# A convolution and two dense layers on one core: five blocks of the first layer ahead of the second, sums kept in DRAM, some additions by DMA

## The chip, the cores and the metric

The kernel runs on 1 core of a Trainium2 chip. The metric is device time in microseconds (us) of one execution; lower is better. The profiled execution has a trace with every instruction of the engines (TensorE or PE, VectorE or DVE, ScalarE or ACT, GpSimd or POOL) and every DMA; SP issues most DMAs. "Granted clock" is the share of TensorE's full clock (2.4 GHz) that it was granted; the lower level is 1.2 GHz.

## The reference

```python
# x: (2, 4096, 192), weight_gen: (2, 4096, 8, 7); w_in: (192, 2048), w_out: (2048, 192), two of each; weights as 64-bit numbers
w = softmax(weight_gen, axis=-1)                       # 7 taps for each of 8 heads of 24 channels
out = einsum('bshk,bskhg->bshg', w, last_7_rows_of_x)  # a causal local sum
x1 = out.reshape(8192, 192)
h = x1 @ w_in1;  x2 = maximum(0.01 * h, h) @ w_out1    # first layer
h = x2 @ w_in2;  r = maximum(h, 0);  return (r * r) @ w_out2   # second layer
```

The x and the weight_gen are float32, the weights come as 64-bit numbers, which the kernel converts itself.

## The kernel before

The 8192 tokens are cut into 16 blocks (`tb`) of 512. Each block goes through a local sum (softmax of the taps, seven products with shifted rows of x, six additions), then the first layer, then the second. A layer is 8 steps (`j`), each for two chunks of 128 hidden units: `mm1` makes the hidden sums of both chunks (18 products, L491), `activate` applies the nonlinearity on ACT and splits the result into a rounded part `gh` and a rest `gl` (DVE, L516), and `mm2` multiplies both with `w_out` (20 products, L533), two steps later (`LAG`). Every operand is such a pair of rounded part and rest, so each product is taken three times. The contraction over 192 channels is done by two halves of the array with 64 rows each; so a block's input is kept as `a` (channels 0 to 127), `b` (channels 128 to 191, twice) and `s` (`a` with its halves swapped), each with its rest: six tiles, `XS`, and three sets of them.

Layers alternate: `phases` is (layer 0, block 0), then (0, 1), (1, 0), (0, 2), (1, 1) and so on. At the end of a first-layer block, `end1` adds the two halves' sums (`total`, ACT copy L554, DVE addition L557), exchanges halves by DMA and makes the six tiles of the second layer at once. At the end of a second-layer block, `end2` adds, transposes and stores the output.

The weights are converted in `piece`: a DMA load of the 64-bit words (`raw`), an ACT scaling (L261), five DVE instructions (L265 to L287) that put the high and the low word together, the last of them the addition of L287, an ACT copy for the rounded part (L299) and a DVE subtraction for the rest (L304). Each matrix is converted in pieces of one or two steps' worth (384 or 768 columns of 128 partitions): five pieces for each first-layer matrix, four for each second-layer one.

`local_sum` for blocks 0 and 1 (`EARLY`) ends in transposes on TensorE into PSUM, three groups (`a`, `b`, `s`); for later blocks it ends in a DVE transpose, a round trip through DRAM (`sc`) and a `swap` by DMA for `s`. Its buffers `xc`, `wg` and `att` exist once.

What sets the order: every operation is entered in a `Plan` with an engine, an estimated cost, a priority (counted in steps), and what it reads and writes. `issue` is a list scheduler that runs once while the program is built: for each engine it takes, among the next 60 by priority, the one that can start first by the estimates (TensorE strictly by priority), and writes the instructions in that order. Each engine then runs its instructions in this fixed order, so one that waits on the chip holds up those behind it. `late` is the estimate for a DMA. Rings (`buf`) are buffers that a plan entry takes when it is issued; `raw` has 2, the wide scratch tiles `w` 4, the tiles `c` 3.

Of the kernel before, what the change touches and what calls it, by code (L numbers as in the profile page):

```python
# [37 lines left out]
class Plan:  # L38
# [10 lines left out]
    def op(self, eng, cost, prio, reads, writes, fn, after=(), late=0.0):  # L49
        deps = set(after)  # L50
        for b in reads:
            deps.update(b.writers)
        for b in writes:
            deps.update(b.readers or b.writers)
        o = Op(eng, cost, fn, prio, deps, [], late)
        for b in dict.fromkeys([*reads, *writes]):
            o.bufs.append(b)
            b.left += 1
        for b in reads:
            b.readers.append(o)  # L60
        for b in writes:
            if b.readers:
                b.writers, b.readers = [], []
            b.writers.append(o)
        self.ops.append(o)
        return o

    def issue(self, gap=0.07):
# [28 lines left out]
        while left:  # L97
# [31 lines left out]
            if o.late:  # L129
                wire = max(wire, s + o.cost) + o.late  # L130
                o.end = wire + 2.0
# [10 lines left out]
def kernel(  # L142
# [17 lines left out]
    nc = tc.nc  # L160
# [20 lines left out]
    LAG = 2  # L181
    EARLY = 2
# [22 lines left out]
    ident_b = Buf()  # L205

# [16 lines left out]
    def piece(kind, l, j, nj, pr):  # L223
        n = nj * 3 * P
        raw = pl.buf(sb, [P, SW, 2], I32, "raw", "raw", 2)
        wu = pl.buf(sb, [P, SW], F32, "wu", "w", 4)
        wa = pl.buf(sb, [P, SW], F32, "wa", "w", 4)
# [5 lines left out]
        if kind == "i":  # L233
            src = (w_in1, w_in2)[l].rearrange("(s p) (n e m) w -> p s n e (m w)", p=Q, e=2, m=P)
            for d in range(2):
# [6 lines left out]
                pl.op("SP", 0.5 * nj, pr - 6, [], [raw], load, late=nj * 0.7)  # L242
        else:
# [7 lines left out]
            pl.op("SP", 0.5, pr - 6, [], [raw], load, late=nj * 1.4)  # L251
# [4 lines left out]
        def I(b):  # L256
# [4 lines left out]
            lambda: nc.scalar.activation(V(wu), raw.t[:, :n, 1].bitcast(F32), AF.Copy, scale=2.0**-112),  # L261
        )
# [34 lines left out]

        hb = Buf()
        pl.op("ACT", act(n), pr - 1, [wa], [hb], lambda: nc.scalar.copy(hi, val()))  # L299
        parts = [(lo, slice(None))] if kind == "i" else [(lo[:, :, Q:], slice(0, P)), (lo[:, :, :Q], slice(P, D))]  # L300
        for to, cs in parts:
            pl.op(
                "DVE", dve(n // len(parts)), pr - 1, [wa, hb], [done],
                lambda to=to, cs=cs: nc.vector.tensor_tensor(  # L304
                    to, val()[:, :, cs], hi[:, :, cs].bitcast(F32), op=ALU.subtract
                ),
            )

# [20 lines left out]
    x1 = []  # L329
    taken = []  # L330

    def swap(xs, pr):
        for k in "hl":
# [6 lines left out]
            pl.op("SP", 1.0, pr, [xs["a" + k]], [xs["s" + k]], go, late=1.0)  # L340

    AW = 5 * Q

    def local_sum(tb, pr, gate=()):
# [5 lines left out]
        xs = x_set()  # L350
        x1.append(xs)
# [3 lines left out]
        def load_w():  # L355
            for i in range(BI):
                nc.sync.dma_start(
# [3 lines left out]
        def load():  # L361
            q = nc.sync if tb else nc.scalar
# [11 lines left out]
        pl.op("SP", 2.0, pr - 10, [], [wg], load_w, after=gate, late=0.4)  # L374
        pl.op(*(("SP", 2.0) if tb else ("ACT", 4.0)), pr - 10, [], [xc], load, after=gate, late=3.6)
# [23 lines left out]
        c0 = Q if tb < EARLY else 0  # L399

        def acc():
            return att.t[:, :, c0 : c0 + D].rearrange("p t (h g) -> p t h g", g=G)
# [6 lines left out]
        for k in range(1, K):  # L409
            tmp = pl.buf(sb, [P, TB, H, G], F32, "tmp", "c", 3)  # L410
            pl.op("DVE", dve(TB * D), pr - 2, [xc, wg], [tmp], lambda k=k, tmp=tmp: prod(k, tmp.t))
            pl.op(
                "DVE", dve(TB * D), pr - 2, [att, tmp], [att],
                lambda tmp=tmp: nc.vector.tensor_tensor(acc(), acc(), tmp.t, op=ALU.add),  # L414
            )

        def halves(k, v, bufs, dep, pr):
            h, lo = xs[k + "h"], xs[k + "l"]
            pl.op("ACT", act(N), pr, [dep], [h], lambda: nc.scalar.copy(h.t, v()))
            pl.op(  # L420
                "DVE", dve(N), pr, [dep, h], [lo],
                lambda: nc.vector.tensor_tensor(lo.t, v(), h.t.bitcast(F32), op=ALU.subtract),
            )

        if tb < EARLY:

            def copies():
                nc.scalar.copy(
                    att.t.rearrange("p t (c e) -> p t c e", e=Q)[:, :, 0:5:4],
                    att.t.rearrange("p t (c e) -> p t c e", e=Q)[:, :, 2:4],  # L430
                )

            pl.op("ACT", act(N), pr - 1, [att], [att], copies)
            for k, o in (("a", Q), ("b", 3 * Q), ("s", 0)):
# [8 lines left out]
                halves(k, lambda pt=pt: pt.t[:, 0, :], None, pt, pr - 1)  # L443
        else:
            J = D // 32
            xb = pl.buf(sb, [P, J, TB, 32], F32, "xb", "c", 3)
# [9 lines left out]
                lambda: nc.sync.dma_start(out=sc.t, in_=xb.t.rearrange("p j t a -> p (j t a)")), late=1.5,  # L456
            )
            for k, js in (("a", (0, 1, 2, 3)), ("b", (4, 5, 4, 5))):
# [9 lines left out]
                pl.op("SP", 2.0, pr - 2, [sc], [v, *xs.values()], back, after=taken[max(tb - 2, 0) : max(tb - 1, 0)], late=1.2)  # L468
                halves(k, lambda v=v: v.t, None, v, pr - 1)
# [3 lines left out]
    x2 = []  # L473
# [4 lines left out]
    def mm1(l, tb, j, pr):  # L478
        xs = (x1, x2)[l][tb]
        ph = h_t[l, tb, j] = pl.buf(ps, [P, 2, N], F32, "ph", "ph", 2)  # L480

        def go():
            wh, wl = wi[l]["h"], wi[l]["l"]
            slots = ("asb", "sab")
            terms = [(wh, "h", s) for s in (0, 1, 2)] + [(wl, "h", s) for s in (0, 1, 2)]
            terms += [(wh, "l", s) for s in (0, 1, 2)]
            for i, (w, hl, s) in enumerate(terms):

                for d in range(2):
                    c = s if d == 0 else (1, 0, 2)[s]  # L490
# [3 lines left out]
                        rhs=xs["asb"[s] + hl].t[HALVES[d]],  # L494
# [66 lines left out]
    def wide(name):  # L561
        return pl.buf(sb, [P, N], F32, name, "w", 4)

    def end1(tb, acc, pr):
        xs = x_set()
        x2.append(xs)
        sa, bs, bw = wide("sa"), wide("bs"), wide("bw")
        taken.append(total(acc, 0, sa, [*xs.values()], pr))
        total(acc, 1, bs, [bw], pr)

        def other():
            nc.sync.dma_start(out=bw.t[0:Q], in_=bs.t[Q:P])
            nc.sync.dma_start(out=bw.t[Q:P], in_=bs.t[0:Q])

        pl.op("SP", 1.0, pr, [bs], [bw], other, late=1.0)
        ah, al, bh, bl = (xs[k] for k in ("ah", "al", "bh", "bl"))
        pl.op("ACT", act(N), pr + 1, [sa], [ah], lambda: nc.scalar.copy(ah.t, sa.t))
        pl.op(
            "DVE", dve(N), pr + 1, [sa, ah], [al],
            lambda: nc.vector.tensor_tensor(al.t, sa.t, ah.t.bitcast(F32), op=ALU.subtract),  # L580
        )
        swap(xs, pr + 1)
        pl.op(
            "DVE", dve(N), pr + 2, [bs, bw], [bs], lambda: nc.vector.tensor_tensor(bs.t, bs.t, bw.t, op=ALU.add)
        )
        pl.op("ACT", act(N), pr + 2, [bs], [bh], lambda: nc.scalar.copy(bh.t, bs.t))
        pl.op(
# [97 lines left out]
```

## Time and profile before

| | us |
|---|---|
| median of 2 runs (1237.59 to 1239.06) | 1238.32 |
| profiled execution, its own time | 1238.8 |
| its span, first to last instruction | 1236.8 |
| TensorE busy | 1163.9 |
| VectorE busy | 741.5 |
| ScalarE busy | 746.6 |
| GpSimd busy | 1.7 |

The span is what the trace covers; the time of the execution is 2.0 us longer. Busy time is an average over stages with different limits: the page's row of 40 slices (30.9 us each) and the windows show each stretch by itself. A wait is listed with who ended it.

### The profile page before, as it was taken

To read this page: it belongs to the slowest core of one execution; us is meant where nothing else is said; L and a number is where in the kernel's file an instruction comes from. 1 tells how busy PE (TensorE), PEld (TensorE's weight loads), DVE (VectorE), ACT (ScalarE), POOL (GpSimd) and SP (SyncE) were. 2 spreads that over 40 slices of the span, in tenths; PEclk is the share of its full clock that TensorE was granted. 3 is DMA by queue.
4 is the path that set the end of the run, shared out by engine and by line. 5 is a ranking of instruction groups with operands and counts; after the bars stand their busy time and mean duration, and the time that the engine had idled before them with its cause. 6 is when DMAs were issued, how large, how long until landed. Compare 5 with 4: busy or idle time off the path is not lost.

```text
span 1236.8 us, 22770 instructions
## 1 busy us (share of the span) xinstructions
PE 1163.9 (94%) x9752; PEld 932.6 (75%) x9752; DVE 741.5 (60%) x886; ACT 746.6 (60%) x826; POOL 1.7 (0%) x7
## 2 busy tenths in 40 slices
PE   1569889999999999999999999999999999999997
PEld 0457668888888787878878787887878788787885
DVE  6899988747383754738374573738456473433333
ACT  1446665765647566564757566475756657475674
POOL 0000000000000000000000000000000000000000
PEclk9879979999999999999999999999999999999999
DMA  4454253321213131122313112131312211111111
GB/s 91 120 127 122 73 119 69 99 51 35 67 35 92 35 92 36 42 51 49 79 35 92 35 48 51 42 79 35 92 35 64 45 32 43 35 27 18 27 18 18
DMA packets 99532, 72.77 MB, mean 59 GB/s; under 512 B 58156, under 2 KB 84810, under 8 KB 99432
## 3 DMA queue, kind: packets, MB, share of 16 engines
q1 hardware_dynamic: 99120, 70.36, 24.6%
q8 instruction: 76, 1.25, 0.4%
q10 hardware_dynamic: 312, 0.97, 0.3%
q14 instruction: 24, 0.20, 0.1%
HBM read 37.47 MB, written 11.80 MB: 40 GB/s over the span
## 4 chain that ended last, share of the span: by engine, by line
PE 91%; DVE 6%; DMA 1%; ACT 1%; issue 0%; SPq 0%; DVEq 0%; ACTq 0%
PE ph L491 43%; PE pa L533 29%; PE pb L533 19%; DVE att L414 1%; DVE tmp L406 1%; DVE gl L516 1%; DMA raw<-in_moe_w_in_dram 1%; DVE wu L281 0%; DVE wa L271 0%; DVE wa L287 0%; DMA xa<-sc 0%; DVE wu L277 0%; DVE wa L265 0%; DMA xc<-in_x_dram 0%; DVE wo L304 0%
## 5 line engine op out<-in xcount | busy, mean ns | idle before, releaser
L516 DVE TENSOR_TENSOR gl<-g,gh 128x1024 fp32r<-128x1024 f32 x256 | 313.3, 1224 | 412.2 <-ACT g L513 273.8
L533 PE MATMUL pa<-gh,wo 64*128 64x512 f32 x2048 | 285.1, 397 | 7.7 <-DVE sa L557 7.7
L508 ACT ACTIVATE gh<-ph 128x1024 fp32r<-128x1024 f32 x128 | 131.6, 1028 | 258.6 <-PE ph L491 258.5
L533 PEld LDWEIGHTS pa<-gh,wo 64*128 64x128 f32 x2048 | 194.1, 186 | 58.0 <-DVE sa L557 8.5
L511 ACT ACTIVATE g<-ph 128x1024 f32<-128x1024 f32 x128 | 131.6, 1028 | 152.3 <-PE ph L491 151.7
L533 PE MATMUL pa<-gl,wo 64*128 64x512 f32 x1024 | 162.8, 395 | 4.1 <-DVE gl L516 4.1
L533 PE MATMUL pb<-gh,wo 64*128 64x512 f32 x1024 | 162.3, 394 | 3.8 <-DVE bs L557 3.8
L533 PE MATMUL pb<-gl,wo 64*128 64x512 f32 x1024 | 162.6, 395 | 0.0
L513 ACT ACTIVATE g<-g 128x1024 f32<-128x1024 f32 x128 | 135.9, 1062 | 3.6
L512 ACT ACTIVATE gh<-g 128x1024 fp32r<-128x1024 f32 x128 | 135.8, 1061 | 3.6
L509 ACT ACTIVATE g<-ph 128x1024 f32<-128x1024 f32 x128 | 130.5, 1020 | 0.5 <-DVE gl L516 0.5
L533 PEld LDWEIGHTS pa<-gl,wo 64*128 64x128 f32 x1024 | 97.3, 186 | 27.6 <-DVE gl L516 4.6
L533 PEld LDWEIGHTS pb<-gh,wo 64*128 64x128 f32 x1024 | 97.2, 186 | 27.4 <-DVE bs L557 4.5
L533 PEld LDWEIGHTS pb<-gl,wo 64*128 64x128 f32 x1024 | 97.5, 186 | 23.3
L414 DVE TENSOR_TENSOR att<-att,tmp 128x768 f32<-128x768 f32 x96 | 91.7, 955 | 2.0
L406 DVE TENSOR_TENSOR tmp<-xc,wg 128x768 f32<-128x768 f32 x96 | 91.3, 951 | 0.0
L491 PE MATMUL ph<-xah,wi0h 64*128 64x512 f32 x256 | 52.8, 408 | 14.5 <-ACT wi0h L299 14.5
L491 PE MATMUL ph<-xah,wi0l 64*128 64x512 f32 x256 | 52.8, 408 | 4.6 <-DVE wi0l L304 4.6
L491 PE MATMUL ph<-xsh,wi0l 64*128 64x512 f32 x256 | 52.3, 404 | 0.0
L491 PE MATMUL ph<-xbh,wi0l 64*128 64x512 f32 x256 | 52.3, 404 | 0.0
L491 PE MATMUL ph<-xsh,wi0h 64*128 64x512 f32 x256 | 52.2, 403 | 0.0
L491 PE MATMUL ph<-xal,wi0h 64*128 64x512 f32 x256 | 52.0, 402 | 0.0
(90 smaller groups left out, 1461.0 us busy)
## 6 DMA issues: line engine op xcount, KB each, us to landing
xc<-in_x_dram SPq DMA_DIRECT2D x60, 240.0 KB, 4.3
xsh<-xah SPq DMA_DIRECT2D x60, 128.0 KB, 2.4
xsl<-xal SPq DMA_DIRECT2D x60, 128.0 KB, 2.4
raw<-in_moe_w_in_dram SPq DMA_DIRECT2D x32, 192.0 KB, 4.0
raw<-in_moe_w_out_dram SPq DMA_DIRECT2D x7, 768.0 KB, 4.5
sc<-xb SPq DMA_DIRECT2D x14, 384.0 KB, 2.4
bw<-bs SPq DMA_DIRECT2D x32, 128.0 KB, 2.3
out_dram<-ta SPq DMA_DIRECT2D x64, 64.0 KB, 2.1
```

The lines of the kernel that those rows point to most:

```text
L406: nc.vector.tensor_tensor(dst, xk, wg.t[:, :, :, k : k + 1].to_broadcast([P, TB, H, G]), op=ALU.mult)
L414: lambda tmp=tmp: nc.vector.tensor_tensor(acc(), acc(), tmp.t, op=ALU.add),
L491: nc.tensor.matmul(ph.t[:, d, :], lhsT=w[HALVES[d], c, j, :], rhs=xs["asb"[s] + hl].t[HALVES[d]], start=(i == 0), stop=(i == len(terms) - 1),)
L508: pl.op("ACT", W, pr, [ph], [gh], lambda: nc.scalar.activation(gh.t, ph.t, AF.Prelu, alpha=0.01))
L509: pl.op("ACT", W, pr, [ph], [g], lambda: nc.scalar.activation(g.t, ph.t, AF.Prelu, alpha=0.01))
L511: pl.op("ACT", W, pr, [ph], [g], lambda: nc.scalar.activation(g.t, ph.t, AF.Relu))
L512: pl.op("ACT", W, pr, [g], [gh], lambda: nc.scalar.activation(gh.t, g.t, AF.Square))
L513: pl.op("ACT", W, pr, [g], [g], lambda: nc.scalar.activation(g.t, g.t, AF.Square))
L516: lambda: nc.vector.tensor_tensor(gl.t, g.t, gh.t.bitcast(F32), op=ALU.subtract),
L533: nc.tensor.matmul(acc[d][w == "b"].t, lhsT=wt[:, {"ah": slice(0, P), "b": slice(P, 2 * P), "al": slice(2 * P, 3 * P)}[w]], rhs=g.t[HALVES ...
```

## The change

1. Order of the layers: `LEAD = 5`. The first five phases are layer 0 of blocks 0 to 4, then (1, 0), (0, 5), (1, 1), (0, 6) and so on; the last five phases are all of layer 1.
2. `end1` only adds and stores the sums to DRAM (`ka`, `kb`). A new `again` reads them back one phase ahead of the second layer (`b` twice by four DMAs in place of the exchange) and makes the six tiles.
3. Second-layer weight tiles are allocated where the first layer's staging buffers (`raw0` with 4, `w0` with 8) were, in a pool that is closed first; so the first write of second-layer weights waits for all of the first layer's conversion (`borrowed`). Second-layer pieces have priorities 16 steps early, and each loads after the piece two before it and starts after the one before it (`gate=one[-2:]`).
4. For all pieces of the first layer but the first of each matrix, the addition of L287 becomes a DMA with `accum_op=ALU.add`, issued by POOL (`plus`); in block 1's local sum so do five of the six additions of L414.
5. Blocks 0 and 1 make `s` by two products with a permutation matrix and two ACT copies (`turn`), in place of the third group of transposes, ACT copy and DVE subtraction.
6. First block: x is loaded by SP and weight_gen by ACT, where it was the other way round. Block 1's local sum has its priority 6 steps ahead of its phase, it was 1.
7. `mm1` takes the terms of `a` and `b` first and those of `s` last. Scratch tiles `c` 2 for 3, the output sums have a ring `e` of their own. The estimates `late` become pairs (time on the wire, further delay) with other values.

The diff, cut to its core:

```diff
+    LEAD = 5
-    wi = [{k: const.tile([P, 3, NPR, P], F32R, name=f"wi{l}{k}") for k in "hl"} for l in range(2)]
-    wo = [const.tile([P, NFC, 2 * D], F32R, name=f"wo{l}") for l in range(2)]
+    weight_tiles(const, 0)
+    stage = ExitStack()
+    sg = stage.enter_context(tc.tile_pool(name="sg", bufs=1))
+    borrowed = []
+    def second():
+        if len(wi) == 1:
+            stage.close()
+            weight_tiles(ctx.enter_context(tc.tile_pool(name="const2", bufs=1)), 1)
+    def plus(to, tv, of, ov, pr, late):
+        pl.op(
+            "POOL", 1.0, pr, [of, to], [to],
+            lambda: nc.gpsimd.dma_start(out=tv(), in_=ov(), accum_op=ALU.add), late=late,
+        )
-    def piece(kind, l, j, nj, pr):
+    def piece(kind, l, j, nj, pr, dma=False, gate=()):
+        pool, rings = (sb, (("raw", 2), ("w", 4))) if l else (sg, (("raw0", 4), ("w0", 8)))
...
-        pl.op(
-            "DVE", dve(n), pr - 2, [wu, wa], [wa],
-            lambda: nc.vector.tensor_tensor(V(wa), V(wa), V(wu), op=ALU.add),
-        )
+        if dma:
+            plus(wa, lambda: V(wa), wu, lambda: V(wu), pr - 2, (nj * 0.8, 4.5))
+        else:
+            pl.op(
+                "DVE", dve(n), pr - 2, [wu, wa], [wa],
+                lambda: nc.vector.tensor_tensor(V(wa), V(wa), V(wu), op=ALU.add),
+            )
+        pl.op("ACT", act(n), pr - 1, [wa], [hb], high, after=tuple(borrowed) if l else ())
...
+    def turn(xs, pe, pr):
+        pt = pl.buf(ps, [P, 2, N], F32, "pt", "ph", 2)
+        for i, k in enumerate("hl"):
+            pl.op(
+                "PE", MM, pe + 0.1 * i, [xs["a" + k], perm_b], [pt],
+                lambda i=i, k=k: nc.tensor.matmul(pt.t[:, i, :], lhsT=perm, rhs=xs["a" + k].t, start=True, stop=True),
+            )
+        for i, k in enumerate("hl"):
+            pl.op("ACT", act(N), pr, [pt], [xs["s" + k]], lambda i=i, k=k: nc.scalar.copy(xs["s" + k].t, pt.t[:, i, :]))
...
-                nc.sync.dma_start(
+                (nc.sync if tb else nc.scalar).dma_start(
                     out=wg.t[i * A : (i + 1) * A].rearrange("p t h k -> p (t h k)"), in_=wg_flat[i, :, tb]
-            q = nc.sync if tb else nc.scalar
+            q = nc.sync
...
+            if tb == 1 and k < K - 1:
+                plus(att, flat, tmp, lambda tmp=tmp: tmp.t.rearrange("p t h g -> p t (h g)"), pr - 2, (1.6, 4.5))
+            else:
+                pl.op(
+                    "DVE", dve(TB * D), pr - 2, [att, tmp], [att],
+                    lambda tmp=tmp: nc.vector.tensor_tensor(acc(), acc(), tmp.t, op=ALU.add),
+                )
...
+            terms = [(w, hl, s) for ss in ("ab", "s") for w, hl in ((wh, "h"), (wl, "h"), (wh, "l")) for s in ss]
...
     def end1(tb, acc, pr):
+        kept[tb] = [pl.buf(dram, [P, N], F32, n, n, LEAD + 2) for n in ("ka", "kb")]
+        for i in range(2):
+            v, to = wide("s", ("e", 2)), kept[tb][i]
+            total(acc, i, v, [], pr)
+            pl.op("SP", 0.5, pr, [v], [to], lambda v=v, to=to: nc.sync.dma_start(out=to.t, in_=v.t), late=(0.8, 2.0))
+    def again(tb, pr, gate):
+        o = pl.op(
+            "SP", 0.5, pr - 2, [ka], [sa, *xs.values()], lambda: nc.sync.dma_start(out=sa.t, in_=ka.t),
+            after=(taken[-1], *gate), late=(0.8, 2.0),
+        )
+        def twice():
+            for v, rows in ((bu, slice(0, Q)), (bl_, slice(Q, P))):
+                for d in range(2):
+                    nc.sync.dma_start(out=v.t[HALVES[d]], in_=kb.t[rows])
+        halves(xs, "a", lambda: sa.t, sa, pr - 1)
+        swap(xs, pr - 1)
+        pl.op(
+            "DVE", dve(N), pr - 1, [bu, bl_], [bu],
+            lambda: nc.vector.tensor_tensor(bu.t, bu.t, bl_.t, op=ALU.add),
+        )
+        halves(xs, "b", lambda: bu.t, bu, pr - 1)
...
-    phases = [(0, 0)]
-    for tb in range(1, NTB):
-        phases += [(0, tb), (1, tb - 1)]
-    phases.append((1, NTB - 1))
+    phases = [(0, tb) for tb in range(LEAD)]
+    for tb in range(NTB):
+        phases.append((1, tb))
+        if tb + LEAD < NTB:
+            phases.append((0, tb + LEAD))
...
-            piece(kind, l, j, n, at[l, 0] + j + (LAG if kind == "o" else 0))
+            o = piece(
+                kind, l, j, n, at[l, 0] + j + (LAG if kind == "o" else 0) - 16 * l, dma=l == 0 and j > 0, gate=one[-2:] if l else ()
+            )
+            if l:
+                one.append(o)
...
-                    local_sum(tb + 1, at[0, tb + 1] - (4 if tb else 1), gate=() if tb == 0 else (starts[0, tb - 1],))
+                    if lq:
+                        again(tq, at[lq, tq] - 3, gate)
+                    else:
+                        local_sum(tq, at[lq, tq] - (4 if tq >= EARLY else 6), gate)
```

## Rows read from the trace of the kernel before

**Rows 1.** The page, parts 1 and 2: busy times, and DVE's forty slices.
```profile
PE 1163.9 (94%) x9752; PEld 932.6 (75%) x9752; DVE 741.5 (60%) x886; ACT 746.6 (60%) x826; POOL 1.7 (0%) x7
...
DVE  6899988747383754738374573738456473433333
```

**Rows 2.** Windows: stretch, length, busy time by engine, granted clock, DMA share, GB/s.
```profile
13.70:100.00 86.30, 47.38 (x288) 35.05 (x288) 78.27 (x111) 33.63 (x43) 0.00 (x0) 0.84 0.45 108
100.00:170.90 70.90, 59.42 (x459) 47.51 (x460) 66.07 (x88) 41.28 (x50) 0.00 (x0) 0.86 0.49 126
250.00:275.00 25.00, 25.00 (x216) 20.08 (x214) 10.56 (x13) 16.03 (x18) 0.00 (x0) 1.00 0.11 21
```

**Rows 3.** TensorE's waits, whole run: waiter, releaser, total us, times, longest us.
```profile
PE pt L440 <- DVE att L414: 26.0, 1, 26.0
PE ph L491 <- ACT wi0h L299: 14.5, 3, 10.8
PE pa L533 <- DVE sa L557: 7.7, 1, 7.7
...
PE pb L533 <- DVE bs L557: 3.8, 1, 3.8
```

**Rows 4.** Timeline (start, length, ...): first product of steps 0, 8, 255; window of L491.
```profile
30.09 0.80 PE L491 MATMUL ph<-xah,wi0h 64*128 64x512 f32 x2
...
100.01 0.79 PE L491 MATMUL ph<-xah,wi0h 64*128 64x512 f32 x2
...
277.86:1218.88 941.02, 479.21 (x3800) 359.05 (x3800) 1.00 0.21 48
...
1218.72 0.40 PE L491 MATMUL ph<-xah,wi1h 64*128 64x512 f32 x2
```

**Rows 5.** Timeline of the first block's loads and DVE's chain of products and additions.
```profile
0.74 1.98 SPq L357 DMA_DIRECT2D wg<-in_weight_gen_dram  x4
3.35 1.03 ACTq L370 DMA_DIRECT2D xc<-in_x_dram  x2
8.67 2.21 ACTq L367 DMA_DIRECT2D xc<-in_x_dram  x2
13.71 0.96 DVE L406 TENSOR_TENSOR att<-xc,wg 128x768 f32<-128x768 f32 x1 [0.88 <-DMA xc<-in_x_dram]
...
24.88 0.96 DVE L414 TENSOR_TENSOR att<-att,tmp 128x768 f32<-128x768 f32 x1
```

**Rows 6.** DMA issues: destination and source, queue, count, KB each, median us to landing.
```profile
xsh<-xah SPq DMA_DIRECT2D x60, 128.0 KB, 2.4
...
raw<-in_moe_w_in_dram SPq DMA_DIRECT2D x32, 192.0 KB, 4.0
raw<-in_moe_w_out_dram SPq DMA_DIRECT2D x7, 768.0 KB, 4.5
...
xc<-in_x_dram ACTq DMA_DIRECT2D x2, 240.0 KB, 3.5
```

**Rows 7.** DVE's groups by line and shape: count, busy us, mean ns, idle before.
```profile
L516 DVE TENSOR_TENSOR gl<-g,gh 128x1024 fp32r<-128x1024 f32 x256 | 313.3, 1224 | 412.2 <-ACT g L513 273.8 <-PE pb L533 135.6 <-ACT g L509 2.4
L414 DVE TENSOR_TENSOR att<-att,tmp 128x768 f32<-128x768 f32 x96 | 91.7, 955 | 2.0
...
L450 DVE STREAM_TRANSPOSE xb<-att 128x768 f32<-128x768 f32 x14 | 13.7, 978 | 0.5
L287 DVE TENSOR_TENSOR wa<-wa,wu 128x768 f32<-128x768 f32 x14 | 13.4, 957 | 0.5
L277 DVE TENSOR_SCALAR wu<-wa 128x768 int32<-128x768 int32 x14 | 7.8, 557 | 0.3
L396 DVE TENSOR_TENSOR wg<-wg,sm 128x224 f32<-128x224 f32 x16 | 6.3, 392 | 0.5
L287 DVE TENSOR_TENSOR wa<-wa,wu 128x384 f32<-128x384 f32 x4 | 2.2, 558 | 0.1
L422 DVE TENSOR_TENSOR xsl<-pt,xsh 128x512 fp32r<-128x512 f32 x2 | 1.4, 684 | 0.0
```

More of the change, by code (lines that the diff above doesn't have):

```diff
@@ L47, in buf, with op @@
         return Buf(lambda i: pool.tile(shape, dtype, name=name, tag=f"{tag}_{i}", bufs=1), (tag, bufs))
-    def op(self, eng, cost, prio, reads, writes, fn, after=(), late=0.0):
+    def op(self, eng, cost, prio, reads, writes, fn, after=(), late=None):
         deps = set(after)
@@ L129, in issue @@
             if o.late:
-                wire = max(wire, s + o.cost) + o.late
-                o.end = wire + 2.0
+                wire = max(wire, s + o.cost) + o.late[0]
+                o.end = wire + o.late[1]
             else:
@@ L240, in load @@
                         nc.sync.dma_start(out=to[:, :, q], in_=src[:, :, j + q, d])
-                pl.op("SP", 0.5 * nj, pr - 6, [], [raw], load, late=nj * 0.7)
+                pl.op("SP", 0.5 * nj, pr - 6, [], [raw], load, late=(nj * 0.6, 3.5), after=gate[:1])
         else:
@@ L249, in load @@
                 )
-            pl.op("SP", 0.5, pr - 6, [], [raw], load, late=nj * 1.4)
+            pl.op("SP", 0.5, pr - 6, [], [raw], load, late=(nj * 1.2, 3.0), after=gate[:1])
         def V(b):
@@ L372, in load @@
                     )
-        pl.op("SP", 2.0, pr - 10, [], [wg], load_w, after=gate, late=0.4)
-        pl.op(*(("SP", 2.0) if tb else ("ACT", 4.0)), pr - 10, [], [xc], load, after=gate, late=3.6)
+        pl.op("SP" if tb else "ACT", 2.0, pr - 10, [], [wg], load_w, after=gate, late=(0.4, 2.0))
+        pl.op("SP", 2.0 if tb else 4.0, pr - 10, [], [xc], load, after=gate, late=(3.6, 2.0))
         def w2():
@@ L466, in back @@
                         )
-                pl.op("SP", 2.0, pr - 2, [sc], [v, *xs.values()], back, after=taken[max(tb - 2, 0) : max(tb - 1, 0)], late=1.2)
-                halves(k, lambda v=v: v.t, None, v, pr - 1)
+                o = pl.op("SP", 2.0, pr - 2, [sc], [v, *xs.values()], back, after=taken[-1:], late=(1.0, 2.0))
+                if k == "a":
+                    taken.append(o)
+                halves(xs, k, lambda v=v: v.t, v, pr - 1)
+        if tb < EARLY:
+            turn(xs, at[0, tb] - 0.3, pr - 1)
+        else:
             swap(xs, pr - 1)
-    x2 = []
     h_t = {}
@@ L559, in total, with wide @@
         return o
-    def wide(name):
-        return pl.buf(sb, [P, N], F32, name, "w", 4)
+    def wide(name, ring=("w", 4)):
+        return pl.buf(sb, [P, N], F32, name, *ring)
+    kept = {}
     def end1(tb, acc, pr):
[L565 to L577, printed above, removed]
+        kept[tb] = [pl.buf(dram, [P, N], F32, n, n, LEAD + 2) for n in ("ka", "kb")]
[3 more added lines that the diff above has]
+            pl.op("SP", 0.5, pr, [v], [to], lambda v=v, to=to: nc.sync.dma_start(out=to.t, in_=v.t), late=(0.8, 2.0))
@@ L578, in end1 @@
         pl.op(
-            "DVE", dve(N), pr + 1, [sa, ah], [al],
-            lambda: nc.vector.tensor_tensor(al.t, sa.t, ah.t.bitcast(F32), op=ALU.subtract),
-        )
[L582 to L587, printed above, removed]
-            "DVE", dve(N), pr + 2, [bs, bh], [bl],
-            lambda: nc.vector.tensor_tensor(bl.t, bs.t, bh.t.bitcast(F32), op=ALU.subtract),
-        )
+            "DVE", dve(N), pr - 1, [bu, bl_], [bu],
@@ L640 @@
         weights("o", 1, (2,) * 4)
-        starts = {}
+        starts = []
         for i in range(len(steps) + LAG):
```

130 lines of the change are left out of this document (76 added, 54 removed).

## The prediction

> **What bounds the kernel now.** I read the page's busy shares first. TensorE is busy 94% of the span, VectorE (DVE) 60%, and the slices of DVE show where those 60% lie: the first seven slices stand at 6 to 9 tenths, those from the ninth on at 3 to 8 [rows 1]. So there are two regimes. The windows say the same with numbers: from 13.7 to 100.0 us DVE is busy 78.27 of 86.30 us and TensorE 47.38, with a granted clock of 0.84 (part of the time at 1.2 GHz); from 100.0 to 170.9 DVE has 66.07 of 70.90; from 250 to 275 TensorE has 25.00 of 25.00 at 2.4 GHz and DVE 10.56 [rows 2]. The list of what TensorE waited for has entries in the first regime alone: 26.0 us for the first block's sum on DVE, 14.5 for converted weights (longest 10.8), 7.7 and 3.8 for the sums that free its accumulators [rows 3].
>
> A step is one pair of hidden chunks of one block, 18 products of L491; there are 256, eight to a block and layer. The first begins at 30.09, step 8 at 100.01, the last (step 255) at 1218.72 [rows 4]. Between 277.86 and 1218.88 lie 3800 products in 941.02 us, 211 steps at 4.46 us: TensorE at its full rate, stalls of block changes included. So the span is 100.0 (to step 8) + 247 x 4.46 = 1101.6 + stalls after step 8 + 18.1 (from 1218.7 to the end) = 1236.8, which leaves 17.1 us of stalls after step 8. The steady part and the tail are not touched; the change can move the 100.0 and the 17.1.
>
> **The change, part by part.** *Loads of the first block.* Before, ACT issues the windows of x, and cannot go on with the softmax until its last issue, at 8.67 + 2.21 us; DVE's chain of 13 products and sums starts at 13.71 [rows 5]. After, SP issues x ahead of all weights and ACT the small weight_gen. SP's first window copy can't go before 3.35 (it follows a memset, as on ACT). Seven issues of about 0.5 us (half of the 1.03 for two) end at 6.8, and 3.5 us from issue to landing for such a copy [rows 6] give 10.3. Bounds: 8.5 if the memset costs nothing; 13.7, no gain, if bandwidth set the landing and not its sharing with the weights issued beside it. I take 10.3: 3.4 us gained. The weights of step 0 are issued behind x and land about 6.8 + 1.2 + 4.0 = 12 [rows 6], and the chain (13.71 to 24.88 for its 13 starts, 0.931 each) covers that; were that cover gone, step 0 would wait for them.
>
> *Work taken from DVE before step 8.* Eight of the ten first-layer weight pieces give their addition (L287) to a DMA on POOL's queue: 2 x 0.558 + 6 x 0.957 = 6.9 us. Block 1 gives five of its six additions (L414) away: 5 x 0.955 = 4.8. The swapped copies of blocks 0 and 1 come from two products with a permutation and two ACT copies, so that DVE's xsl falls away: 2 x 0.684 = 1.4 [rows 7]. Together 13.0 us. Also, block 1's sum is now due 6 steps ahead and not 1, so it comes before the last w_out piece, which mm2 wants only after step 8; before, that piece and two gl (4.9 + 2.4 = 7.4 us of DVE) ran ahead of step 8. I count half of it, 3.7, as a gain, since DVE takes whatever is ready; bounds 0 and 7.4. The added turn products (four of the size of an L491 product; two of those take 0.40 [rows 4]) and the ACT copies replace transposes and copies of like size: nothing, covered by TensorE's waits for DVE in this stretch; without the cover 1 us.
>
> Sum: DVE sets step 8. Before, 86.3 us from the chain's start to step 8; after, 86.3 - 13.0 - 3.7 = 69.6; from 10.3 on that is 80. Bounds 76 and 87 (nothing from the earlier loads, nor from the order).
>
> *The additions by DMA.* Thirteen transfers of 196 to 393 KB, SBUF to SBUF, each read-add-write; no row shows one. From below, the swap of a half tile, 128 KB from SBUF to SBUF, lands in 2.4 us; from above, 768 KB of weights take 4.5, and an addition reads twice 384 KB [rows 6]. I take 4.5, for that row has as many bytes read. For the weights this is latency that DVE fills with the next piece (four pieces in flight after, two before). Block 1's five are in series, each waits in POOL's queue for the one before, and every weight addition queued behind it waits too; products wait for a free tmp of two. Block 1's loads can go when block 0's chain ends (10.3 + 12.1 = 22.4); eight issues at 0.5 and 3.5 to landing make 30, and with DVE's other work between I let the chain start near 35; it ends at 35 + 5 x 4.5 = 57.5, and with the last sum, transposes and halves (5.2 us from 24.88 to 30.09 for block 0) [rows 4, 5] at 63. Step 8 at 80 leaves 17 us: up to 7.9 us for one addition costs nothing.
>
> A rule stands against this. What the rows show: L277 does 768 elements in 0.557 us and L287 in 0.957, so the former runs at about two elements a cycle [rows 7]. The Trainium skill (SBUF — State Buffer, "SBUF: two separate sides") says that a DMA issued from GpSimd is starved of descriptors while DVE runs such a mode, and gives 3.1 us in place of 0.62 (under "A bandwidth-pool intuition that's wrong"); by that, an estimate, 2.5 us more for each transfer, 7.0 in place of 4.5, and the sum would stay what it is. By the rows: each addition waits at worst for the two L277-like instructions of one piece, 1.1 us, so 5.6 us, under 7.9. The slow addition is a rival below.
>
> *Order of the layers.* Second-layer weights are needed from step 40 and not from step 16. DVE's load from step 8 to step 48, by [rows 7]: gl 40 x 1.224 = 49.0; two sums for each of five blocks 6.8; four local sums at 17.1 (six small ones at up to 0.392, 13 x 0.955, 0.978, 2 x 0.684) 68.4; the first block read back 3 x 0.684 = 2.1; eight pieces of second weights at 4.94 (two like L277, four like L287) 39.5; left over from block 0 6.4. Sum 172.2 us against 40 x 4.46 = 178.4 of TensorE: it just fits. But the pieces are given priorities 16 steps early. Work due by step 32 is 6.4 + 23 gl 28.2 + 4.1 + 51.3 + 39.5 = 129.5, and DVE does in 24 steps 107.0 x 0.955/0.931 = 109.8: 19.7 us too much if all eight pieces are done by then, 9.8 if two slip past (each waits for the one before, and passes ACT twice). Stalls: 0 to 19.7; I take 10, about the case with two late, against 17.1 before.
>
> *Sums through DRAM.* Per block 512 KB more written and 768 KB read back in place of a 256 KB copy, and some 3 more SP issues of 0.5 us; they have a block's 35.7 us, and the DMA share from 250 to 275 is 0.11 [rows 2]. Nothing, hidden by the steady products; if late, a block start slips by its 2.4 us.
>
> Sum: 80 + 1101.6 + 10 + 18.1 = 1209.7 of span. The profiled run took 1238.8 with a span of 1236.8, and is 0.5 above the median: 1209.7 + 2.0 - 0.5 = 1211.
>
> **Rivals.** *B: the early second weights crowd out gl and the sums.* Place: steps 22 to 36; price: all of the 19.7, and half of the 17.1 that waits for operations put in an order that came out late cost before, 28 in all: 80 + 28 + 1101.6 + 18.1 + 1.5 = 1229. For it: the 7.7 and 3.8 us waits of before came from just such an order [rows 3]. Against: the load as a whole fits. *C: it all fits.* Step 8 at 76 and no stall: 1197. For it: the 172.2 against 178.4; against: before, DVE idled 8 us of 86 even where it was the bound [rows 2]. *D: the additions are slow*, the other side: place is POOL's queue before step 8. If POOL comes to prepare a transfer only in DVE's gaps, 8.0 us in 86.3 [rows 2], one that needs 0.6 us of them waits 6.5, and an addition takes 11.0. Beyond 7.9 us, five in series push step 8 by 5 us for each us: at 11.0 it is 1227, at 13.3 the gain is gone, and from 18.3 on the kernel is over 2% slower (step 8 at 132, 1263). For it: DVE is busy nine tenths of this stretch; against: 18.3 is four times the row for as many bytes. The Trainium skill's page named above has such a lock, for those of DVE's instructions that run at the double rate.
>
> **How the numbers follow.** A measurement of this kernel can tell about 2% from no change, that is below 1213.5 or above 1263. Chances: the forecast 0.48 (its own range 1200 to 1222; 0.33 below 1213.5, 0.15 above), B 0.20 (within), C 0.17 (faster), D 0.15 (0.08 within, 0.07 slower). Faster 0.50, within 2% 0.43, slower 0.07. For 8 in 10 the range reaches from C's lower part, 1195, to past B, 1232, and leaves out D's upper part and the tails.
>
> **What would show it.** L287 is left with 10 instructions in place of 18; 13 additions stand on POOL's queue, each 3 to 6 us to landing. The first product on DVE starts at 10.3 (8.5 to 13.7), the first L491 at 26.7, the 145th (step 8) at 80. After it TensorE waits about 10 us, most of it between steps 22 and 40 for gl or the sums of L557; from step 48 on no wait. Wrong if: TensorE's long waits before step 8 end with a POOL transfer; DVE shows idle time waiting for one; waits appear at block changes of the second layer, for data read back; or the tail is not 18.

## The result and the profile after

The changed kernel takes 1189.83 us (median; 1188.75 to 1190.91): 0.961 of the time before [0.956, 0.965]. That is 21 us below the forecast and 5 below its range. The profiled execution took 1188.75, its span is 1187.0. In the changed kernel L549 is `mm1`, L591 `mm2`, L574 the `gl` subtraction, L320 the weights' addition left on DVE, L333 the copy of converted weights, L247 the issue of an addition by DMA.

The page after, parts 1 and 2, to be read against [rows 1]:

```profile
PE 1139.3 (96%) x9748; PEld 919.8 (77%) x9748; DVE 725.3 (61%) x871; ACT 749.3 (63%) x830; POOL 15.7 (1%) x20
...
DVE  7999999848465474745648475564846543344333
```

Practically as many products as before take TensorE 24.6 us less (1163.9 before). Work that only starts earlier does not do that: either the clock or the pace of a product is another. The windows of both traces part the two: 17.5 of the 24.6 us lie between steps 40 and 255, where the granted clock is 1.00 in both kernels, and 4.9 between steps 8 and 40, where it is 0.94 before and 1.00 after.

TensorE's waits after, to be read against [rows 3]:

```profile
PE pt L496 <- DVE att L483: 21.6, 1, 21.6
PE ph L549 <- ACT wi0h L333: 8.9, 3, 3.7
PE ph L549 <- DVE wi0l L343: 2.5, 1, 2.5
PE pt L391 <- DVE xal L406: 2.2, 2, 1.2
PE pa L591 <- DVE s L615: 1.9, 2, 1.0
PE ph L549 <- DVE xbl L406: 0.9, 1, 0.9
PE pa L591 <- DVE gl L574: 0.6, 1, 0.6
```

The first block comes 4.4 us sooner. The waits for the sums that free the accumulators (`sa` and `bs` of L557, now `s` of L615) go from 11.5 to 1.9 us, those for `wi0h` from 14.5 to 8.9, with 3.7 as the longest in place of 10.8.

The timeline after: the first product of step 0, of step 8, of two neighbouring steps of the first layer and two of the second, the last of them step 255; then the window from step 40 to step 255 (of L549 alone: stretch, length, busy PE and PEld, granted clock, DMA share, GB/s), to be read against [rows 4]:

```profile
25.66 0.80 PE L549 MATMUL ph<-xah,wi0h 64*128 64x512 f32 x2
...
81.51 0.50 PE L549 MATMUL ph<-xah,wi0h 64*128 64x512 f32 x2
...
121.67 0.40 PE L549 MATMUL ph<-xah,wi0h 64*128 64x512 f32 x2
126.12 0.40 PE L549 MATMUL ph<-xah,wi0h 64*128 64x512 f32 x2
...
1164.81 0.39 PE L549 MATMUL ph<-xah,wi1h 64*128 64x512 f32 x2
1169.12 0.39 PE L549 MATMUL ph<-xah,wi1h 64*128 64x512 f32 x2
...
227.61:1169.12 941.51, 479.94 (x3871) 363.20 (x3870) 1.00 0.26 66
```

A first-layer step takes 126.12 - 121.67 = 4.45 us, as every step did before. A second-layer step takes 1169.12 - 1164.81 = 4.31, at a granted clock of 1.00 in both. From step 40 to 255 lie 88 steps of the first layer and 127 of the second: 941.51 - 88 x 4.46 leaves 4.32 for one of the second. So 127 x 0.14 = 18 us came from a part that the forecast held fixed.

What can set the pace of a product with the same instruction, shape and clock? The change moves the second layer's weights to another place in SBUF. By the program's own addresses, in bytes within a partition: before, all weight tiles start at 128 within 512 bytes (17024, 29312 and so on) and all moving operands (the x tiles, `gh`, `gl`) at 288. After, the first layer's weights are still at 128 and the moving operands at 288, but the second layer's weights start at 288 too (180000, 192288, 204576), high in the partition. Every slice that a product reads lies a multiple of 512 bytes from its tile's start, so a whole layer has one distance.

### The profile page after: what moved, and what is told of

It reads as the page before. It is cut to its first block, busy times and chain, and to the rows that moved or that the text cites. A ratio compares the mean times of both kernels' runs of the same rounds, so it can differ in the third digit from the quotient of the medians.

```text
span 1187.0 us, 22999 instructions
## 1 busy us (share of the span) xinstructions
PE 1139.3 (96%) x9748; PEld 919.8 (77%) x9748; DVE 725.3 (61%) x871; ACT 749.3 (63%) x830; POOL 15.7 (1%) x20
## 4 chain that ended last, share of the span: by engine, by line
PE 90%; DVE 6%; issue 1%; ACT 1%; DMA 1%; SPq 0%; POOL 0%; DVEq 0%; POOLq 0%; ACTq 0%
PE ph L549 43%; PE pa L591 29%; PE pb L591 19%; DVE gl L574 1%; DVE tmp L471 1%; DVE att L483 1%; DVE wa L301 1%; DVE wu L311 0%; DVE wu L307 0%; DVE wa L295 0%; DMA xc<-in_x_dram 0%; DVE wo L343 0%; DMA wg<-in_weight_gen_dram 0%; ACT wu L290 0%; DMA bw<-ob 0%
## 5 line engine op out<-in xcount | busy, mean ns | idle before, releaser
L574 DVE TENSOR_TENSOR gl<-g,gh 128x1024 fp32r<-128x1024 f32 x256 | 312.7, 1223 | 391.0 <-ACT g L571 292.7
L591 PE MATMUL pa<-gh,wo 64*128 64x512 f32 x2048 | 280.3, 392 | 2.0 <-DVE s L615 1.9
L591 PEld LDWEIGHTS pa<-gh,wo 64*128 64x128 f32 x2048 | 191.5, 185 | 50.0 <-DVE oa L615 3.5
L591 PE MATMUL pa<-gl,wo 64*128 64x512 f32 x1024 | 159.9, 390 | 0.6 <-DVE gl L574 0.6
L591 PE MATMUL pb<-gh,wo 64*128 64x512 f32 x1024 | 159.9, 390 | 0.0
L591 PE MATMUL pb<-gl,wo 64*128 64x512 f32 x1024 | 159.5, 389 | 0.0
L591 PEld LDWEIGHTS pa<-gl,wo 64*128 64x128 f32 x1024 | 96.1, 184 | 22.9 <-DVE gl L574 1.1
L591 PEld LDWEIGHTS pb<-gh,wo 64*128 64x128 f32 x1024 | 96.1, 184 | 22.3 <-DVE wo L343 0.5
L591 PEld LDWEIGHTS pb<-gl,wo 64*128 64x128 f32 x1024 | 96.2, 184 | 21.9
L483 DVE TENSOR_TENSOR att<-att,tmp 128x768 f32<-128x768 f32 x91 | 86.9, 955 | 1.7
L549 PE MATMUL ph<-xah,wi0h 64*128 64x512 f32 x256 | 52.4, 405 | 8.9 <-ACT wi0h L333 8.9
L549 PE MATMUL ph<-xah,wi0l 64*128 64x512 f32 x256 | 52.4, 405 | 2.5 <-DVE wi0l L343 2.5
L549 PE MATMUL ph<-xbl,wi0h 64*128 64x512 f32 x256 | 51.8, 401 | 0.9 <-DVE xbl L406 0.9
L549 PE MATMUL ph<-xbh,wi0l 64*128 64x512 f32 x256 | 51.9, 402 | 0.0
L549 PE MATMUL ph<-xbh,wi0h 64*128 64x512 f32 x256 | 51.6, 400 | 0.0
L549 PE MATMUL ph<-xal,wi0h 64*128 64x512 f32 x256 | 51.6, 399 | 0.0
```

The costliest lines, as they stand in the source:

```text
L549: nc.tensor.matmul(ph.t[:, d, :], lhsT=w[HALVES[d], c, j, :], rhs=xs[s + hl].t[HALVES[d]], start=(i == 0), stop=(i == len(terms) - 1),)
L574: lambda: nc.vector.tensor_tensor(gl.t, g.t, gh.t.bitcast(F32), op=ALU.subtract),
L591: nc.tensor.matmul(acc[d][w == "b"].t, lhsT=wt[:, {"ah": slice(0, P), "b": slice(P, 2 * P), "al": slice(2 * P, 3 * P)}[w]], rhs=g.t[HALVES ...
```

## The experiments

### Where the second layer's pace comes from

Four kernels with nothing but unused bytes between tiles, so with the same instructions in the same order:

```diff
 # b_w32: the kernel before                      # b_x0: the line behind warm alone
     ident_b = Buf()
+    const.tile([P, 8], F32, name="pad0")
     ...
     warm = const.tile([P, 1], F32, name="warm")
+    const.tile([P, 8], F32, name="pad1")
 # a_w32: the same two lines in the changed kernel
 # a_w0: the changed kernel
+            c2 = ctx.enter_context(tc.tile_pool(name="const2", bufs=1))
+            c2.tile([P, 8], F32, name="pad2")
+            weight_tiles(c2, 1)
```

> The kernel before, with 32 unused bytes per partition ahead of the weights and 32 behind them: all weights of both layers start at 32 within 64 bytes instead of 0 (160 within 512), the moving operands stay at 32 within 64 (352 within 512). Nothing else changes: same instructions, same order. Theory address (the start of the weights within 64 bytes sets the pitch of a step): every step 4.31 us instead of 4.45, 256 x 0.14 = 36 us less, about 1203 us, ratio 0.971. Theory region (the high end of the partition, where the change puts the second layer's weights, is quicker to read): 1238, ratio 1.000. Theory 512 (weights and moving operands have to start at the same place within 512 bytes): 1238. Theory schedule (what runs beside the second layer's steps in the changed kernel makes them quick): 1238.

> The kernel before with 32 unused bytes per partition behind the weights only: the weights stay at 0 within 64 bytes, the moving operands go from 32 to 0. Theory address, of the weights alone: pitch 4.45, 1238 us, ratio 1.000. Theory same phase (weights and moving operands at the same place within 64 bytes, as they are in the changed kernel's second layer): pitch 4.31, about 1203, ratio 0.971. Theory moving (the moving operands' place alone counts): any pitch but 4.45. Theories region and schedule: 1238.

> The changed kernel with 32 unused bytes ahead of the second layer's weights, which then start at 0 within 64 bytes as the first layer's do; same region, same order of work. Theory address: the second layer's steps go back to 4.45, 128 x 0.14 = 18 us more, about 1208 us, ratio to the kernel before 0.975; this would be what the new order is worth by itself, close to the sum that was forecast. Theories region and schedule: 1190, ratio 0.961.

> The changed kernel with the first layer's weights also at 32 within 64 bytes (32 unused bytes ahead of them and 32 behind), the rest where it was within 64 bytes. Theory address: the first layer's 128 steps go from 4.45 to 4.31 too, 18 us less, about 1172 us, ratio 0.947. Theories region and schedule: 1190, ratio 0.961.

Measured: b_w32 1234.06 us, 0.9965 [0.9955, 0.9976]; b_x0 1233.76, 0.9966 [0.9954, 0.9978]; a_w0 1204.97, 0.974 [0.972, 0.976]; a_w32 1187.96, 0.960 [0.959, 0.962]. The place of the weights within 64 bytes is not it: b_w32 won 4 us of 36, a_w32 2 of 18. An equal place within 64 bytes is not it either: b_w32 (both at 32) and b_x0 (both at 0) have it, at a pitch of 4.43. Nor is it the region or the schedule: a_w0 moves the second layer's weights by 32 bytes in the same region, and their steps go from 4.31 to 4.43. What the quick steps have in common, here and in a_w32, is that weights and moving operands start at the same place within 512 bytes. The next four test that:

```diff
 # b_d0, b_d256, b_d128: the kernel before
     warm = const.tile([P, 1], F32, name="warm")
+    const.tile([P, n // 4], F32, name="pad1")       # n = 352, 96, 224
 # a_d0: the changed kernel
+    small = ctx.enter_context(tc.tile_pool(name="small", bufs=1))
     const = ctx.enter_context(tc.tile_pool(name="const", bufs=1))
     ...
-        mx = pl.buf(sb, ...);  warm = const.tile(...)
+        mx = pl.buf(small, ...);  warm = small.tile(...)
```

> The kernel before with 352 unused bytes behind the weights: weights and moving operands both start at 128 within 512 bytes (before: 128 and 288). The kernels seen so far, by the distance from weights to moving operands within 512 bytes: 160 gives a pitch of 4.45 us, 192 gives 4.43, 0 (the changed kernel's second layer) gives 4.31; and 480 in the same high region gives 4.43. Theory equal place (distance 0 within 512 is quick, wherever the weights lie): all 256 steps at 4.31, 36 us less, about 1202 us, ratio 0.971. Theory region too (distance 0 helps only with the weights at the high end of the partition, behind the moving operands): 1234 to 1238, ratio 0.997 to 1.000. Theory schedule (something in the changed kernel's second-layer phases): the same.

> The kernel before with 96 unused bytes behind the weights: weights at 128 and moving operands at 384 within 512 bytes, distance 256. If what counts is the place within 256 bytes or less: pitch 4.31, about 1202 us, ratio 0.971. If it is the place within 512 bytes or more: pitch 4.43 to 4.45, 1234 to 1238, ratio 0.997 to 1.000.

> The kernel before with 224 unused bytes behind the weights: weights at 128 and moving operands at 0 within 512 bytes, distance 384. If what counts is the place within 128 bytes: pitch 4.31, about 1202 us, ratio 0.971. If within 256 or 512 bytes: 1234 to 1238, ratio 0.997 to 1.000.

> The changed kernel with two small tiles (32 and 128 bytes) moved ahead of the first layer's weights, which then start at 288 within 512 bytes as the moving operands and the second layer's weights do; nothing else moves. Theory equal place: the first layer's steps go from 4.45 to 4.31 too; of its 128 steps some twenty lie in the stretch before step 8 and in the waits up to step 34, so 110 to 120 x 0.14 = 15 to 17 us less, about 1173 us, ratio 0.947. Theories region and schedule: 1188 to 1190, ratio 0.960.

Measured: b_d0 1201.92 us, 0.971 [0.970, 0.973]; b_d256 1203.53, 0.972 [0.971, 0.974]; b_d128 1229.67, 0.9935 [0.992, 0.995]; a_d0 1174.44, 0.949 [0.947, 0.951]. Equal places are quick wherever the weights lie, and it is the place within 256 bytes that counts. a_d0 beats both kernels.

The groups by line and shape, from 400 to 1100 us, of the kernel before, of b_d0, of b_d0_wi (below, one line number later) and of b_d128: groups of second products (`wo`) and, in the first three, one of first products (`wi0l`). The last figure ahead of the second bar is the mean in ns; in b_d256 it is 386 in these groups, as in b_d0:

```profile
L533 PE MATMUL pa<-gl,wo 64*128 64x512 f32 x628 | 99.0, 393 | 0.0
L533 PE MATMUL pb<-gl,wo 64*128 64x512 f32 x628 | 99.0, 393 | 0.0
L491 PE MATMUL ph<-xbh,wi0l 64*128 64x512 f32 x160 | 31.7, 393 | 0.0
```
```profile
L533 PE MATMUL pa<-gl,wo 64*128 64x512 f32 x648 | 99.8, 386 | 0.0
L533 PE MATMUL pb<-gl,wo 64*128 64x512 f32 x648 | 99.8, 386 | 0.0
L491 PE MATMUL ph<-xbh,wi0l 64*128 64x512 f32 x164 | 31.9, 386 | 0.0
```
```profile
L534 PE MATMUL pa<-gl,wo 64*128 64x512 f32 x638 | 100.7, 392 | 0.0
L534 PE MATMUL pb<-gl,wo 64*128 64x512 f32 x636 | 100.3, 392 | 0.0
L492 PE MATMUL ph<-xbh,wi0l 64*128 64x512 f32 x158 | 30.9, 386 | 0.0
```
```profile
L533 PE MATMUL pa<-gl,wo 64*128 64x512 f32 x632 | 99.1, 391 | 0.0
```

b_d0_wi gives the equal place to the weights of `mm1` alone (32 unused bytes ahead of `wo`, 320 behind `warm`).

> The kernel before with unused bytes such that the moving operands and the weights of a step's first products (wi) start at 128 within 256 bytes, but the weights of the second products (wo) at 160. Theory own pair (each product is quick if its own two operands start at the same place within 256): 9 of 19 pairs of products at the quick 0.2267 us, 10 at the 0.2333 of a pitch of 4.43: pitch 4.37, 0.08 x 256 = 20 us less than before, about 1218 us, ratio 0.984. If one unequal pair spoils all: 4.43, 1234, ratio 0.997. If only the first products count: 4.31, 1202, ratio 0.971.

Measured: 1221.91 us, 0.986 [0.985, 0.988]; pitch 4.38. The first products are at 386 ns, the second at 392, in one and the same step: each product goes by its own two operands. All pitches, from the starts of steps in the timelines:

| weights, moving operands (within 512) | distance within 256 | pitch, us | seen in |
|---|---|---|---|
| 128, 128; 288, 288; 352, 352 | 0 | 4.31 | b_d0; after and a_d0; a_w32, second layer |
| 128, 384 | 0 | 4.31 | b_d256 |
| 128, 0 | 128 | 4.42 | b_d128 |
| 160, 352; 128, 320 | 192 | 4.43 | b_w32, a_w32; b_x0 |
| 320, 288 | 224 | 4.43 | a_w0, second layer |
| 128, 288 | 160 | 4.45 | before; after, first layer |

(The distance is from weights up to moving operands. Only multiples of 32 bytes were tried, and of those not 32, 64 and 96.)

### What the parts of the change are worth

Each of these undoes one part of the changed kernel. First the thirteen additions, back on DVE:

```diff
-            if tb == 1 and k < K - 1:
+            if False:
-    ... dma=l == 0 and j > 0
+    ... dma=False
```

> The changed kernel with all thirteen additions back on DVE instead of POOL's queue (eight of the first layer's weights, five of block 1's sum); turn products, loads and order stay. The forecast's term: 6.9 + 4.8 = 11.7 us of DVE work come back ahead of step 8, which the additions' landing times (5.5 to 6.7 us in the changed kernel, under the 7.9 that would be free) cost nothing in exchange: step 8 at 81.5 + 11.7 = 93 us, 1201 us, ratio 0.970. Rival (what DVE saves it loses waiting for the transfers, five of them in series): step 8 at 80 to 84, 1188 to 1192, ratio 0.961.

Measured: 1200.50 us, 0.970 [0.969, 0.971]; 10.7 us behind the changed kernel, where 11.7 was forecast. Step 8 comes at 89.8 (8.3 later), and steps 11 and 12 are 3.6 and 1.0 us longer than the pitch, with a wait of 2.8 us for `gl`: DVE's work left over. The transfers' landing times in the changed kernel, by the table of DMA issues (count, KB each, median us; the single ones land after 4.2 to 7.6):

```profile
wa<-wu POOLq DMA_DIRECT2D x6, 384.0 KB, 6.3
att<-tmp POOLq DMA_DIRECT2D x5, 384.0 KB, 6.7
...
wa<-wu POOLq DMA_DIRECT2D x2, 192.0 KB, 5.5
```

Then the first block's loads, back on their queues (x on ACT's, weight_gen on SP's):

> The changed kernel with the first block's x issued from ACT's queue again and weight_gen from SP's. The forecast's term, 3.4 us: DVE's chain starts at 13.7 in place of 9.3, and step 8 comes 3.4 to 4.4 us later, 1193 to 1194 us, ratio 0.964. Rival (DVE makes good the later start with weight pieces that are ready, so the order of the loads is worth nothing by step 8): 1190, ratio 0.961.

Measured: 1203.80 us, 0.973 [0.971, 0.975]: 14.0 us, four times the forecast's term. The timeline of a_oldq, ACT's queue and DVE's first product, and the window from 10 to 15 us (columns as in [rows 2]):

```profile
4.14 2.37 ACTq L436 DMA_DIRECT2D xc<-in_x_dram  x2
...
10.37 3.76 ACTq L436 DMA_DIRECT2D xc<-in_x_dram  x2
14.69 2.04 ACTq L433 DMA_DIRECT2D xc<-in_x_dram  x2
...
22.97 0.96 DVE L471 TENSOR_TENSOR att<-xc,wg 128x768 f32<-128x768 f32 x1 [4.08 <-DMA xc<-in_x_dram]
...
10.00:15.00 5.00, 0.00 (x0) 0.00 (x0) 0.00 (x0) 0.00 (x0) 0.00 (x0) 1.00 1.14 226
```

DVE's chain starts at 22.97, not at the 13.71 of before [rows 5]. From 10 to 15 us no engine works and the DMA engines are full (share 1.14): weights, of which more pieces are now fetched ahead, move at the same time, and two issues on ACT's queue take 3.76 us. Two kernels with two pieces ahead, with the new and the old order of loads, tell whether that is it:

```diff
-        pool, rings = ... else (sg, (("raw0", 4), ("w0", 8)))
+        pool, rings = ... else (sg, (("raw0", 2), ("w0", 4)))
```

> The changed kernel with two of the first layer's weight pieces fetched ahead, as in the kernel before, in place of four; the loads of x first, as changed. Theory crowding: with x ahead of the weights it makes no difference to the start of DVE's chain, 9.3; the additions by DMA now have fewer pieces in flight to hide behind, so step 8 comes 0 to 6 us later: 1190 to 1196, ratio 0.961 to 0.966.

> As a_two, with the first block's x on ACT's queue again and weight_gen on SP's, as in the kernel before. Theory crowding (x was late by 13.7 us because four pieces of weights were moving at the same time): with two pieces the chain starts at about 13.7 as in the kernel before, 4 to 5 us behind a_two, ratio to a_two 1.004. Rival (something else in the changed kernel makes ACT's queue slow): the chain starts near 23 as in the kernel with four pieces and the old queues, 14 us behind a_two, ratio to a_two 1.012.

Measured: a_two 1211.48 us, 0.978 [0.976, 0.979]; a_two_oldq 1219.68, 0.9845 [0.983, 0.986]. The chain starts at 9.39 and at 17.77: with two pieces the old order costs 8.4 us at the chain and 8.2 at the end, with four 13.7 and 14.0. Neither theory had 17.77. A count made afterwards, from the order of SP's issues in the program, fits all three starts with the old order: four of the first eight issues of `w_in` are for the second layer's first piece, which has staging of its own in the change and is fetched at once. So ahead of the chain's start the kernel before moves 4 x 192 KB of weights and starts at 13.71 [rows 5], a_two_oldq 8 x 192 and starts at 17.77, a_oldq 12 x 192 + 384 and starts at 22.97: each further 768 KB costs some 3.5 to 4 us, if x is not ahead of them. So the crowding is borne out by the two starts with fewer weights, and its size comes from a count over three kernels that no further run tested. And a_two is a plain miss: two staged pieces in place of four cost 21.7 us, not 0 to 6. TensorE's longest entry of waits in a_two (8.9 in the changed kernel), then ACT's waits for additions in a_two from 9 to 104 us, and those of the changed kernel from 9 to 82:

```profile
PE ph L549 <- ACT wi0h L333: 30.3, 4, 12.4
```
```profile
ACT wi0h L333 <- DMA wa<-wu: 17.1, 4, 8.3
...
ACT wo L333 <- DMA wa<-wu: 6.3, 3, 3.3
```
```profile
ACT wi0h L333 <- DMA wa<-wu: 3.3, 2, 2.9
...
ACT wo L333 <- DMA wa<-wu: 0.3, 1, 0.3
```

With two pieces in flight the additions' latency lies open: ACT waits 23.4 us for it, 3.6 with four, and TensorE's waits for `wi0h` behind it grow by 21.4, which is what the kernel loses. The deeper staging is what hides the additions. (What staging is worth with the additions on DVE was not run.)

The order of the layers and the head start of the second layer's weights:

```diff
 # a_lead2
-    LEAD = 5
+    LEAD = 2
 # a_lead2 and a_late
-    ... at[l, 0] + j + (LAG if kind == "o" else 0) - 16 * l
+    ... at[l, 0] + j + (LAG if kind == "o" else 0)
```

> The changed kernel with the kernel before's order of layers (two blocks of the first layer ahead, then one of each in turn) and so the second layer's weights due from step 16, without the 16 steps' head start that would put them ahead of the first layer's. All else stays: additions by DMA, loads, sums through DRAM, places in SBUF within 512 bytes. The forecast's term: the order takes the stalls after step 8 from 17.1 to 10; with the 3.5 read in the changed kernel it is 13.6 us, so 1203 us with stalls of about 17, ratio 0.972, by waits for wi1h and the sums around steps 16 to 20. Rival (the stalls of before came from DVE's work left over at step 8, which the additions by DMA and the loads already took away, so the order is worth little): 1190 to 1193.

> The changed kernel with the second layer's weights due when they are needed (steps 40 to 50) and not 16 steps earlier. The forecast took it that the early due times cause the stalls after step 8 (10 us forecast, 3.5 read at steps 18, 32 and 34), since DVE's 172.2 us of work by step 48 fit into TensorE's 178.4: without them 0 to 3.5 us less, 1186 to 1190 us, ratio 0.960. Rival (the head start is what keeps the second weights from being late): a wait for wi1h at step 40 or wo1 at 42, some 5 to 15 us as the 10.8 of before, 1195 to 1205, ratio 0.965 to 0.973.

Measured: a_lead2 1208.62 us, 0.976 [0.975, 0.978], 18.8 behind the changed kernel; a_late 1197.03, 0.967 [0.966, 0.969], 7.2 behind. TensorE's longest waits for weights in a_lead2 and in a_late:

```profile
PE pa L591 <- ACT wo L333: 15.0, 1, 15.0
```
```profile
PE pa L591 <- ACT wo L333: 6.7, 1, 6.7
```

In a_lead2 step 18 takes 21.96 us (18.55 before). The long step of before is back in its place, but with another wait: before, step 18 waits for the sums of L557 (7.7 and 3.8 [rows 3]), in a_lead2 for the second layer's converted `w_out`, which is due at step 18. So the order is worth more than the 13.6 us expected, the wait was not among those named, and the rival (worth little) is refuted. In a_late the long step is 44 (13.84), for a later piece of the same matrix; the waits at steps 32 and 34 are gone there. So the head start costs about 2.4 us in those two steps and saves 9.5 in step 44: it is not the large source of stalls that the forecast made of it, and the rival's reading (it keeps the second weights from being late) is the right one. Step 44 is longer by more than its wait of 6.7 because the products behind the wait run at a granted clock of 0.50, the lower level, from 252.0 to 257.2 us. The long step 18 of before has that too: its two waits are 11.5 of the 14.1 us that it is too long, and the clock from 155 to 171 us is 0.60.

## Why the prediction was wrong

| term | forecast | measured |
|---|---|---|
| start of step 8 | 80 | 81.5 |
| 247 steps | 1101.6 (4.46 each) | 1084.0 |
| stalls after step 8 | 10 | 3.6 (steps 18, 32, 34) |
| end, from step 255 | 18.1 | 17.9 |
| span | 1209.7 | 1187.0 |

**The step that failed** is the sentence "The steady part and the tail are not touched". It was taken from the instructions: the same products, the same shapes, the same clock. But the change moves the second layer's tiles (point 3 of its list), and a product's pace hangs on where its two operands lie against each other (386 ns against 391 to 393 by the groups above). 17.6 of the 22.7 us between forecast and measured span are this term. With the equal place taken away (a_w0) the changed kernel needs 1205 us, 6 below the forecast and inside its range. With the equal place in both kernels (a_d0 1174.4, b_d0 1201.9) the change in the schedule is worth 27.5 us; between the kernel before and a_w0 it is 33.5, of which some 2 are the second layer's pitch of 4.43 in place of 4.45. So the two effects nearly add up. The forecast's gain was 27, and that this agrees with 27.5 is luck in part: 14.5 us of it come by step 8 (97.6 in b_d0, 83.1 in a_d0), where the forecast had 20, and some 12 behind it, where it had 7.

**The stalls after step 8** were over-sized, 10 for 3.6. DVE is nearly as full there as forecast, 100.55 of the 108.05 us from step 8 to step 32 by the windows, yet no wait for `gl` is left behind step 8 (the 0.6 us in the list are at 52 us). By the forecast's own balance two late pieces cost 9.8 us; in the trace three of the eight copies of second-layer weights come after step 32, which by the same balance (one more piece, 4.9 us) leaves 4.9. The waits there are 0.9 and 1.0 us for the sums of L615 (steps 18 and 34) and 0.9 for `xbl` (step 32), not a crowd of `gl` (rival B). Rival C had no stall but step 8 at 76: its 1197 is nearest, for another reason than its own.

**Step 8** was right in sum. The chain starts at 9.3 (10.3 forecast), the first L549 product comes at 25.7 (26.7), and from the chain to step 8 are 72.2 us (69.6), of which DVE works 68.1. Two errors offset each other in it: before, DVE worked 78.3 of the 86.3 us [rows 2], so its work fell by 10.2 and not by 13.0 + 3.7 = 16.7, while its idle time, which the sum left at 8.0, fell to 4.1. The parts behind the sum are less independent than it made them. The additions by DMA are worth 10.7 (11.7 forecast) with four pieces staged; with two, ACT's waits for them grow by 19.8 us. The loads in new order are worth 14.0 in this kernel and not 3.4, because the pieces fetched ahead would crowd them. 3.4 was right as a difference of the two kernels (13.7 to 9.3 is 4.4), not as the part's own worth. Undone singly, additions, loads, staging and order of layers (with the head start) cost 10.7 + 14.0 + 21.7 + 18.8 = 65 us, about twice what the schedule gains: they lean on each other.

**The additions' time**, 4.5 us, was too low: medians of 5.5 to 6.7, the longest 7.6, still under the 7.9 that were free, so rival D didn't come. The Trainium skill (SBUF — State Buffer, "SBUF: two separate sides") led to an estimate of 7.0, and the trace is nearer to that than to my row; whether DVE's double-rate instructions are what delays them, as the Trainium skill has it, no run here shows. Block 1's five in series took from 37.8 (first issue) to 71.2 us (the last one was issued at 66.1 and landed after 5.1), 33 us where 22.5 were forecast, and came out just in time: in step 7, which holds block 1's transposes and turn products, TensorE's one wait is 1.2 us for `xal`.

**Sums through DRAM** cost nothing, as forecast: no wait in the list has them, and the second-layer phases run at their pitch from their third step on. (The first two take 4.38 to 4.40, because `mm2` is two steps behind and still works with the first layer's weights.)

## What to carry to other kernels

Where TensorE sets the pace (shown here for one shape, the float32 pairs of 64 rows named below), put the weights and the moving operand of a product at the same place within 256 bytes of a partition, and look at the pitch of a step for each class of operands in the timeline, since a change that only moves tiles can change it. "Same instructions, same clock" is not enough to call a part untouched: compare the addresses too. A deep prefetch, the order of loads and latency-bound additions by DMA are one part, not three; price them together, and undo each singly to see which leans on which.

## What the runs showed of the hardware

- A pair of products (64 rows in each half of the array, 128 columns of weights, 512 of float32 moving data) takes 4.31 / 19 = 0.2268 us where weights and moving operand start at the same place within 256 bytes, 0.233 at distances of 128, 192 and 224 and 0.234 at 160: 3% of the whole kernel for 352 unused bytes (b_d0). Why, no row shows; the weight loads' mean changes by 1 ns only (185 before, 184 in b_d0).
- An accumulating DMA from SBUF to SBUF issued by POOL lands after 4.2 to 7.6 us in the changed kernel (medians 5.5 for 192 KB, 6.3 and 6.7 for 384 KB) and after 3.9 to 11.8 us in a_two, where the median for 192 KB (6.9) is above those for 384 KB (6.4 and 5.3); a plain copy of 128 KB lands after 2.4 us [rows 6].
- While weights fill the DMA engines (share 1.08 to 1.14 from 5 to 20 us in a_oldq), two DMA issues on ACT's queue take up to 3.76 us, against 1.03 and 2.21 in [rows 5].
- Behind a wait of 6.7 us TensorE's products ran at a granted clock of 0.50 for 5 us (a_late, 252.0 to 257.2), though the clock was 1.00 in the steady steps.
